# A float16 FFN, plain float32 scores and host-laid inputs in a block-causal attention and gated conv FFN kernel

## The chip, the cores and the metric

The kernel runs on one core of one Trainium2 chip. Its engines are PE (matmul; PEld is its weight load), DVE (vector), ACT (scalar), POOL (GpSimd) and SP, which only issues transfers. The metric is the device time of one execution in microseconds. PE's granted clock is shown in the profile as a share of full speed.

## The reference, cut

```python
# q, k, v: (8 batches, 8 heads, 576 rows, 64);  w_in 512 x 1024, conv_w 3 x 1024, w_out 1024 x 512
scores = scale * np.matmul(q, k.transpose(0, 1, 3, 2))
mask = block_i >= block_j            # blocks of 64 rows: a row sees its own block and those before
scores = np.where(mask, scores, -1000000000.0)
attn = np.exp(scores - max); attn = attn / (sum + 1e-09)
x = (attn @ v), heads side by side   # (8, 576, 512)
h = np.maximum(x @ w_in, 0.0)
conv_out[:, s] = sum over k of conv_w[k] * h[:, s + k - 1]      # zero rows at both ends
gate = 1.0 / (1.0 + np.exp(-conv_out))
return h * gate @ w_out              # (8, 576, 512)
```

The weights arrive as float64 words, so the kernel itself decodes them into float32.

## The kernel before, in words

One program runs on one core. A helper class, `Plan`, first collects every operation (`pl.op`) with its engine, an assumed duration, what it depends on and a target number from a table; `Plan.order` then writes each engine's operations in the order of these numbers, and puts fill matmuls (`work`, L2038) into PE's waits. All eight PSUM banks are given out by it. In it, an operation of DVE marked `port=True` (operands in SBUF) and one of POOL are never planned at the same time.

Heads go in pairs, four to a batch, 32 in all. Batch 0 is done in two parts: "A" (the first 256 rows) and "B" (the rest), both with plain float32 scores (L1477, L1538, L1315), masks by PE (L1481, L1542), and V's product in L1719. The other 28 pairs go whole, with these stages:

- `load_nat` and `load_v`: q, k and v by SP's queue, 64 numbers of a head and row at a time.
- `stage_t`: PE turns q and k (L1166; L1224 in part A), ACT writes the high part in fp32r (L1179, corner of q L1192), DVE the low part (L1182, L1195).
- `stage_s`: three fp32r products per tile (L1391), ACT writes the mask into the bank (L1404), DVE takes maxima (L1413), ACT the exponentials (L1416). `last_s` does the last 64 rows of both heads (L1318, L1321, L1334). `two_planes` writes the normed weights as float16 high (POOL L1271, ACT L1273) and low planes (DVE L1276; for the first tile POOL L1280, L704, L1286). SP turns the planes by transfer (L1297).
- `load_v`: each pair's V is scaled by a power of two, from a sum by ACT (L809), spread by POOL (L812), summed over rows by PE (L815), DVE (L818, L823); then POOL scales it and writes its float16 parts (L829, L704, L835).
- `pair_pv`: the product with V in float16 (L1781), 66 matmuls, two heads side by side; ACT and DVE evict it as high and low parts of x in fp32r (L1789, L1792).
- `ffn`: per batch 8 blocks of w_in, in three products of high and low fp32r parts: FFN-in matmuls (L1824), relu (ACT L1841), the three taps (ACT L1844, DVE L1848, DVE L1852 or ACT L1857 and POOL L1861), tanh (ACT L1864), the gate product (DVE L1867), its high part (ACT L1871 or POOL L704) and low part (POOL L1877), and FFN-out (L1910), evicted by ACT (L1918). A whole batch has two halves, so 16 gate products. A batch's FFN lies beside the attention of the next one.
- `split`: decodes each weight block (DVE L969 to L997) and parts it, for most with two matmuls by an identity (L1048, L1051) and an addition by DVE (L1054). Each block is split as it comes.

## Time and profile before

| | us |
|---|---|
| median of 3 runs (lowest, highest) | 714.97 (714.72, 715.11) |
| span of the profiled execution | 711.6 |
| PE busy | 689.4 |
| DVE busy | 600.5 |
| ACT busy | 589.8 |
| POOL busy | 476.0 |

The span is that of the one profiled execution, from its first to its last instruction. Busy time is the union of an engine's instructions; the chain of waits goes back from the last instruction and says, for each stretch, which engine's work ended last. Matmuls overlap, so the cost of one is the distance between two starts.

### The profile page before, as it was taken

Reading aid. Unit: us, or ns where it says so; the run is one execution under the profiler, and the core shown is the slowest. Engines: PE = TensorE matmul, PEld = TensorE weight load, DVE = VectorE, ACT = ScalarE, POOL = GpSimd, SP = SyncE. Lnnn points to the kernel's source line nnn. Section 1 sums busy time; section 2 is a strip of 40 time slices with the busy share of each in tenths; the row PEclk is TensorE's granted clock in tenths of the full one; section 3 lists DMA queues with packets and bytes.
Section 4 is the critical chain, followed back from the end, with each engine's and each line's share of the span. In section 5 each row is a group of like instructions: output and inputs, shape, how many; then the busy total and the mean of one; then the engine's idle time right before and its main releaser. Section 6 shows DMA issues by size and latency. Waiting matters only on the chain.

```text
span 711.6 us, 17406 instructions
## 1 busy us (share of the span) xinstructions
PE 689.4 (97%) x5824; PEld 575.2 (81%) x5824; DVE 600.5 (84%) x1553; ACT 589.8 (83%) x1859; POOL 476.0 (67%) x716
## 2 busy tenths in 40 slices
PE   8899999998999999999999999999899999999998
PEld 6567778777889788887978888897778879888987
DVE  5999989998888979999988898888998888994441
ACT  6889989897979779798979889997888779884753
POOL 2545285665877758778787758877676767775543
PEclk9999999999999999999999999999999999999999
DMA  8845437699667794957866796877877595574001
GB/s 212 249 101 140 127 63 156 133 184 169 135 133 133 132 178 93 187 111 168 129 133 132 127 183 122 156 143 123 155 125 143 106 192 113 102 141 85 17 29 45
DMA packets 313197, 94.35 MB, mean 133 GB/s; under 512 B 302461, under 2 KB 307605, under 8 KB 313109
## 3 DMA queue, kind: packets, MB, share of 16 engines
q1 hardware_dynamic: 307812, 84.47, 62.1%
q10 hardware_dynamic: 5296, 8.78, 3.8%
q8 instruction: 46, 0.75, 0.4%
q14 instruction: 43, 0.34, 0.2%
HBM read 37.38 MB, written 9.44 MB: 66 GB/s over the span
## 4 chain that ended last, share of the span: by engine, by line
PE 56%; DVE 17%; ACT 16%; issue 3%; POOL 3%; SPq 2%; DMA 2%; ACTq 0%; POOLq 0%; DVEq 0%
PE bank L1910 19%; PE bank L1824 17%; PE bank L1391 5%; PE bank L1781 4%; PE bank L1719 3%; DVE ptbl L1276 3%; DVE su L1413 3%; PE bank L1166 2%; PE bank L1318 2%; ACT t L1864 2%; ACT t L1844 2%; DVE t L1848 2%; ACT bank L1841 1%; DVE t L1867 1%; DVE h L1276 1%
## 5 line engine op out<-in xcount | busy, mean ns | idle before, releaser
L1824 PE MATMUL bank<-x,wih 128*128 128x290 f32 (+3 forms) x1024 | 195.0, 302 | 4.0 <-DVE t L1867 1.8
L1824 PEld LDWEIGHTS bank<-x,wih 128*128 128x128 f32 x1024 | 153.6, 188 | 15.2 <-DVE t L1867 4.3
L1877 POOL TENSOR_TENSOR gl<-t,gh 128x289 fp32r<-128x289 f32 (+3 forms) x128 | 107.7, 845 | 43.0 <-ACT gh L1871 36.9
L1910 PE MATMUL bank<-woh,gh 128*128 128x512 f32 (+1 forms) x296 | 120.0, 406 | 0.1
L1910 PE MATMUL bank<-woh,gl 128*128 128x512 f32 (+1 forms) x296 | 114.8, 388 | 0.0
L1910 PE MATMUL bank<-wol,gh 128*128 128x512 f32 (+1 forms) x296 | 114.5, 387 | 0.0
L1824 PE MATMUL bank<-x,wil 128*128 128x290 f32 (+3 forms) x512 | 108.6, 298 | 0.0
L1413 DVE TENSOR_REDUCE su<-bank 128x1 f32<-128x384 f32 (+3 forms) x224 | 101.2, 481 | 6.7 <-ACT bank L1404 5.9
L1848 DVE SCALAR_TENSOR_TENSOR t<-bank,cw,t 128x286 f32<-128x286 f32 (+3 forms) x128 | 65.4, 512 | 21.9 <-ACT t L1844 18.5
L1824 PEld LDWEIGHTS bank<-x,wil 128*128 128x128 f32 x512 | 81.1, 188 | 1.5 <-issue 0.7
L1867 DVE SCALAR_TENSOR_TENSOR t<-t,bank 128x289 f32<-128x289 f32 (+3 forms) x128 | 56.6, 448 | 16.4 <-ACT t L1864 15.1
L1844 ACT ACTIVATE t<-bank,cw 128x287 f32<-128x287 f32 (+3 forms) x128 | 63.6, 499 | 4.7 <-POOL gl L1877 2.2
L1910 PEld LDWEIGHTS bank<-woh,gh 128*128 128x128 f32 x296 | 55.6, 188 | 13.6 <-issue 3.6
L1910 PEld LDWEIGHTS bank<-woh,gl 128*128 128x128 f32 x296 | 55.6, 188 | 12.1
L1864 ACT ACTIVATE t<-t 128x289 f32<-128x289 f32 (+3 forms) x128 | 55.6, 444 | 10.3 <-DVE t L1852 4.8
L1910 PEld LDWEIGHTS bank<-wol,gh 128*128 128x128 f32 x296 | 55.8, 188 | 7.2
L1841 ACT ACTIVATE bank<-bank 128x288 f32<-128x288 f32 (+3 forms) x128 | 51.2, 403 | 9.7 <-PE bank L1824 9.0
L1271 POOL TENSOR_SCALAR ptbl<-p3f,su 128x512 f16<-128x512 f32 x56 | 43.9, 792 | 11.6 <-DVE su L1436 8.3
L1861 POOL TENSOR_TENSOR t<-t,ptah 128x287 f32<-128x287 f32 (+1 forms) x28 | 25.1, 898 | 39.1 <-DVE t L1848 20.9
L1391 PE MATMUL bank<-kh,qh 64*128 64x384 f32 (+3 forms) x224 | 43.7, 375 | 2.8 <-DVE x L1792 1.5
L1276 DVE SCALAR_TENSOR_TENSOR ptbl<-p3f,su,ptbl 128x512 f16<-128x512 f32 x56 | 46.0, 829 | 0.1
L1416 ACT ACTIVATE p3f<-bank,su 128x512 f32<-128x512 f32 x56 | 38.2, 684 | 6.8 <-DVE su L1413 6.6
(206 smaller groups left out, 1864.3 us busy)
## 6 DMA issues: line engine op xcount, KB each, us to landing
out_dram<-stage ACTq DMA_DIRECT2D x33, 256.0 KB, 3.4
vn<-in_v_dram SPq DMA_DIRECT2D x58, 128.0 KB, 2.8
qnf<-in_q_dram SPq DMA_DIRECT2D x56, 128.0 KB, 2.7
knf<-in_k_dram SPq DMA_DIRECT2D x56, 128.0 KB, 2.8
x<-in_moe_w_out_dram SPq DMA_DIRECT2D x8, 512.0 KB, 3.7
gh<-in_moe_w_in_dram SPq DMA_DIRECT2D x4, 512.0 KB, 5.5
gl<-in_moe_w_in_dram SPq DMA_DIRECT2D x4, 512.0 KB, 4.3
qtf<-in_k_dram SPq DMA_DIRECT2D x32, 32.0 KB, 2.6
```

What stands on the lines that cost most here:

```text
L1271: nc.gpsimd.tensor_scalar(out=hi(), in0=c(tb.ap), scalar1=st.ap[:, col:col + 1], scalar2=0.0, op0=ALU.mult, op1=ALU.add)
L1276: nc.vector.scalar_tensor_tensor(out=lo(), in0=c(tb.ap), scalar=st.ap[:, col:col + 1], in1=hi(), op0=ALU.mult, op1=ALU.subtract)
L1391: nc.tensor.matmul(home[z][hh].ap[:, cols(i)], t[q_].ap[r, 128 * i:128 * i + 128], t[k_].ap[r, 64 + 128 * (3 - i):S], start=(n == 0), stop ...
L1413: nc.vector.tensor_reduce(out=st.ap[:, k:k + 1], in_=sb.ap[:, cols(i)], op=ALU.max, axis=AX.X, negate=True)
L1824: nc.tensor.matmul(fb.ap[:, 0:n2], wt[:, c, fs], xs[c][xi].ap[:, x0:x0 + n2], start=(n + c - c0 == 0), stop=(n + c - c0 == 3 * NCC - 1))
L1841: nc.scalar.activation(out=fb.ap[:, 0:n2], in_=fb.ap[:, 0:n2], func=AF.Relu, scale=0.5 if b == 0 else 2.0 ** -17)
L1844: nc.scalar.activation(out=t.ap[:, 0:no], in_=fb.ap[:, own:own + no], func=AF.Copy, scale=cw[:, NFC + f:NFC + f + 1])
L1848: nc.vector.scalar_tensor_tensor(out=t.ap[:, i0:no], in0=fb.ap[:, own + i0 - 1:own + no - 1], scalar=cw[:, f:f + 1], in1=t.ap[:, i0:no], o ...
L1864: nc.scalar.activation(out=t.ap[:, 0:no], in_=t.ap[:, 0:no], func=AF.Tanh)
L1867: nc.vector.scalar_tensor_tensor(out=t.ap[:, 0:no], in0=t.ap[:, 0:no], scalar=1.0, in1=fb.ap[:, own:own + no], op0=ALU.add, op1=ALU.mult)
L1877: nc.gpsimd.tensor_tensor(out=gbuf[1].ap[:, f, carry:carry + no], in0=t.ap[:, 0:no], in1=gbuf[0].ap[:, f, carry:carry + no], op=ALU.subtract)
L1910: nc.tensor.matmul(fb.ap[:, 0:cut], gbuf[a].ap[:, f, cs], w[:, f, ds], start=(f == 0 and n == 0), stop=(f == NFC - 1 and n == 2))
```

## The change

All six inputs are laid out by the host before the launch: q and k turned, a pair's two heads on 128 partitions, with q's last block of both heads as a block diagonal of 128 columns; v with 640 columns a row; the weights by block. So PE turns nothing for q and k, and a pair's q, k or v comes in one transfer. All scores are plain float32 with PE writing the mask; x, both weights and the gated h are float16 high and low parts; a factor for w_in, one for w_out and one for V of each batch keep them in range. The factor of V is taken per batch by DVE's maximum of each pair (L774), that of each weight over all its eight blocks (L918), so a block is decoded when it comes and split (`split_w`) when the scale is there. Operations may name other engines (`other`); the table's last two bits choose one. The planner lets DVE's `port` operations and POOL's overlap, at a longer duration (`BESIDE`).

```diff
+    BESIDE = 0.4
-                if o.port:
-                    t = max(t, port)
+            if o.port:
+                o.end += self.BESIDE * max(0.0, min(o.end, port[e != POOL]) - t)
+                port[e == POOL] = o.end
...
-    NX = 7
+    NX = 8
-    wih = cp.tile([P, NCC, DFF], F32R, tag="wih", name="wih")
+    wih = cp.tile([P, NCC, DFF], F16, tag="wih", name="wih")
...
     def load_qk(p, at, part=None):
+                eng.dma_start(out=x.ap[:, c], in_=src[b, z, :, c])
...
     def stage_t(nat, at):
+        (xq, lq), (xk, lk) = nat
+        o = scale_q(xq, slice(0, QW), at, lq, POOL)
+        return {"q": xq, "k": xk}, [o, lk], [o, lk]
...
     def stage_s(ops, at):
-                        for n, (q_, k_) in enumerate((("qh", "kh"), ("qh", "kl"), ("ql", "kh"))):
-                            for hh in range(2):
-                                r = slice(64 * hh, 64 * hh + 64)
-                                nc.tensor.matmul(home[z][hh].ap[:, cols(i)], t[q_].ap[r, 128 * i:128 * i + 128],
-                                                 t[k_].ap[r, 64 + 128 * (3 - i):S], start=(n == 0), stop=(n == 2))
+                        for hh in range(2):
+                            r = slice(64 * hh, 64 * hh + 64)
+                            nc.tensor.matmul(home[z][hh].ap[:, cols(i)], t["q"].ap[r, 128 * i:128 * i + 128],
+                                             t["k"].ap[r, 64 + 128 * (3 - i):S], start=True, stop=True)
+                    for hh in range(2):
+                        r = slice(64 * hh, 64 * hh + 64)
+                        x = home[z][hh].ap[0:64, 0:128 * len(tiles)].rearrange("p (j c) -> p j c", c=128)[:, :, 64:128]
+                        nc.tensor.matmul(x, rident[r, r], maskt[r, :].unsqueeze(1).broadcast_to([64, len(tiles), 64]), start=False, stop=True,
+                                         skip_group_check=True)
...
     def load_v(b, at):
+                nc.vector.tensor_reduce(out=sc.ap[:, z:z + 1], in_=vn.ap.rearrange("p c j d -> p (c j d)"), op=ALU.max, axis=AX.X,
+                                        apply_absolute_value=True)
     def split_v(p, at):
+            nc.vector.scalar_tensor_tensor(out=piece(1), in0=src(), scalar=sc.ap[:, 6:7], in1=piece(0), op0=ALU.mult,
+                                           op1=ALU.subtract)
...
     def scale_w(k, at):
+        o, o1 = sums(wm, 16 * k, NFC, at, [wraw[f][2] for f in range(NFC * k, NFC * k + NFC)], [])
     def split_w(f, at):
+        s_, d = ((lambda: fac.ap[:, 2:3]), wdone["a"]) if k == 0 else ((lambda: wm.ap[:, 26:27]), wdone["o"])
+            nc.scalar.activation(out=hi, in_=src(), func=AF.Copy, scale=s_())
+            nc.vector.scalar_tensor_tensor(out=lo, in0=src(), scalar=s_(), in1=hi, op0=ALU.mult, op1=ALU.subtract)
...
     def two_planes(tb, c, n, st, col, hi, lo, bufs, at, deps, pool):
+            return a, pl.op(POOL, c_pool(n, True), h2p, at + 0.6, deps=[a], bufs=[tb, *bufs],
+                            other=((DVE, c_dve(n, two_in=True), partial(h2p, nc.vector), True),))
...
     def ffn(b, o0, o1, xs, at, span):
-            rl = o = pl.op(ACT, c_act(n2) + 0.04, relu, clock, deps=[o, wdone["cw"]], bufs=[fb])
+            rl = o = pl.op(ACT, c_act(n2) + 0.04, relu, clock, deps=[o], bufs=[fb], other=((DVE, c_dve(n2), relu_v),))
-            gdone.append(pl.op(POOL, c_pool(no, True), c6, clock + 3.5, deps=[o] + prev_tail, bufs=[t]))
+            gdone.append(pl.op(POOL, c_pool(no, True), c6, clock + 3.5, deps=[o] + prev_tail, bufs=[t],
+                               other=((DVE, c_dve(no, two_in=True), partial(c6, nc.vector), True),)))
```

PE, scores of a pair of batch 1, before (kh, kl, qh, ql are high and low parts of k and q):

```order
L1391 MATMUL bank<-kh,qh 128x128 x2
L1391 MATMUL bank<-kl,qh 128x128 x2
L1391 MATMUL bank<-kh,ql 128x128 x2
L1391 MATMUL bank<-kh,qh 128x256 x2
L1391 MATMUL bank<-kl,qh 128x256 x2
L1391 MATMUL bank<-kh,ql 128x256 x2
L1391 MATMUL bank<-kh,qh 128x384 x2
L1391 MATMUL bank<-kl,qh 128x384 x2
L1391 MATMUL bank<-kh,ql 128x384 x2
```

PE, the scores of such a pair after (maskt is the mask, rident an identity):

```order
L1171 MATMUL bank<-k,q 128x128 x2
L1171 MATMUL bank<-k,q 128x256 x2
L1177 MATMUL bank<-maskt,rident 64x2x64 x2
L1171 MATMUL bank<-k,q 128x384 x2
L1177 MATMUL bank<-maskt,rident 64x64 x2
L1171 MATMUL bank<-k,q 128x512 x2
L1177 MATMUL bank<-maskt,rident 64x64 x2
```

Three products per tile have become one, and PE's mask matmuls stand behind each bank's tiles.

DVE near the program's start, before (gh is a decoded w_in block, wil its low part, st holds maxima of the first scores):

```order
L997 SCALAR_TENSOR_TENSOR wil<-gh 128x4x128
L1570 TENSOR_REDUCE st_151<-st_151 128x4
L990 TENSOR_SCALAR gh<-gh 128x512
L1574 RECIPROCAL st_151<-st_151 128x4
L997 SCALAR_TENSOR_TENSOR wil<-gh 128x4x128
L1054 TENSOR_TENSOR wil<-bank,gh 128x4x128
L1753 TENSOR_TENSOR x<-bank,x 64x256
```

DVE there after, where the last w_in maximum (wm) is taken and the scale is made:

```order
L1334 TENSOR_REDUCE st_150<-bank 128x1 x2
L1348 TENSOR_REDUCE st_148<-st_148 128x4
L881 SCALAR_TENSOR_TENSOR wf<-raw,wf 128x512
L1352 RECIPROCAL st_148<-st_148 128x4
L1281 TENSOR_REDUCE st_144<-st_144 128x2
L719 TENSOR_REDUCE vs<-bank 128x1
L918 TENSOR_REDUCE wm<-raw 128x1
L1286 RECIPROCAL st_144<-st_144 128x2
L724 TENSOR_SCALAR vs<-vs 128x1
L709 TENSOR_REDUCE wm<-wm 128x1
L734 TENSOR_SCALAR wm<-wm 128x1
L884 TENSOR_SCALAR raw<-wf 128x512
```

The low part of a block no longer follows its decoding; the maxima, the scale and softmax maxima of batch 0 stand between.

POOL, V's scale and parts for a pair of a later batch, before (vn is V as loaded, vs its scale, vx its float16 parts):

```order
L812 TENSOR_SCALAR dg<-ident,vs 128x128
L704 TENSOR_SCALAR gh<-t 128x287
L1877 TENSOR_TENSOR gl<-t,gh 128x287
L829 TENSOR_SCALAR vn<-vn,vs 128x640
L704 TENSOR_SCALAR vx<-vn 128x640
L835 TENSOR_TENSOR vx<-vn,vx 128x640
```

POOL there after (vb takes V's parts, p0f and p1f are exponentials, ptbl the planes):

```order
L813 TENSOR_SCALAR vb<-vn,vs 128x640
L1055 TENSOR_SCALAR p1f_110<-p1f_110,su_158 128x256
L1055 TENSOR_SCALAR p0f_106<-p0f_106,su_158 128x128
L1061 TENSOR_SCALAR ptbl<-p1f_110 128x2x128
L1061 TENSOR_SCALAR ptbl<-p1f_112 128x2x128
L1061 TENSOR_SCALAR ptbl<-p0f_106 128x128
L1045 TENSOR_SCALAR ptbl<-p2f_116,su_158 128x3x128
L1067 TENSOR_TENSOR ptbl<-p0f_106,ptbl 128x128
```

One pass over V is left on POOL, and the second tile's planes have come to it from ACT and DVE.

## Rows read from the trace of the kernel before

**Rows 1.** The page: busy us and share by engine; shares of the chain

```profile
PE 689.4 (97%) x5824; PEld 575.2 (81%) x5824; DVE 600.5 (84%) x1553; ACT 589.8 (83%) x1859; POOL 476.0 (67%) x716
...
PE 56%; DVE 17%; ACT 16%; issue 3%; POOL 3%; SPq 2%; DMA 2%; ACTq 0%; POOLq 0%; DVEq 0%
```

**Rows 2.** Busy us by engine and stretch; PE clock, DMA share, GB/s

```profile
0.00:20.00 20.00, 17.78 (x101) 12.51 (x102) 11.22 (x41) 13.70 (x41) 6.52 (x17) 1.00 0.82 211
20.00:36.00 16.00, 13.65 (x77) 7.86 (x76) 15.60 (x43) 13.92 (x45) 8.73 (x14) 1.00 0.87 249
...
60.00:140.00 80.00, 78.88 (x552) 60.62 (x551) 75.68 (x201) 73.18 (x230) 46.41 (x69) 1.00 0.56 125
...
400.00:480.00 80.00, 80.00 (x728) 69.14 (x728) 70.63 (x193) 71.46 (x233) 59.82 (x91) 1.00 0.79 150
480.00:560.00 80.00, 75.79 (x700) 64.67 (x697) 72.34 (x180) 66.79 (x215) 58.59 (x90) 1.00 0.72 132
```

**Rows 3.** Timeline of DVE, 32nd and 112th gate product; start, length

```profile
245.77 0.46 DVE L1867 SCALAR_TENSOR_TENSOR t<-t,bank 128x289 f32<-128x289 f32 x1 [0.24 <-ACT t L1864]
...
647.32 0.82 DVE L1867 SCALAR_TENSOR_TENSOR t<-t,bank 128x289 f32<-128x289 f32 x2
```

**Rows 4.** Chain of waits in the tail; start, length, what

```profile
658.48 12.88 PE bank L1824 x96
```

**Rows 5.** Timeline of PE in a steady cycle; start us, length us, engine, line

```profile
412.97 0.37 PE L1166 MATMUL bank<-rident,knr 128*128 128x128 f32 x3
413.18 0.47 PE L1910 MATMUL bank<-woh,gh 128*128 128x512 f32 x1
413.48 0.40 PE L1910 MATMUL bank<-wol,gh 128*128 128x512 f32 x1
413.72 0.40 PE L1910 MATMUL bank<-woh,gl 128*128 128x512 f32 x1
...
415.21 0.55 PE L1781 MATMUL bank<-ptbh,vv 128*64 128x256 f16 x8
415.59 0.32 PE L1781 MATMUL bank<-t,vv 128*64 128x64 f16 x10
```

**Rows 6.** Chain of waits, steady: fp32r scores of a pair, last block

```profile
415.92 2.10 PE bank L1391 x24
...
448.19 0.99 PE bank L1318 x6
```

**Rows 7.** Timeline of PE in the head, plain float32 scores and masks

```profile
46.60 1.13 PE L1477 MATMUL bank<-kh,qh 64*128 64x512 f32 x4
...
47.69 0.50 PE L1048 MATMUL bank<-wih,nident 128*128 128x512 f32 x1
```

**Rows 8.** Chain of waits in the head

```profile
36.07 0.74 PE bank L1824 x4
...
61.78 1.17 PE bank L1315 x4
...
64.04 3.18 PE bank L1719 x16
```

**Rows 9.** DVE groups by line and shape; busy us, mean ns

```profile
L1413 DVE TENSOR_REDUCE su<-bank 128x1 f32<-128x512 f32 x56 | 37.5, 683 | 2.5 <-ACT bank L1404 2.4
...
L1276 DVE SCALAR_TENSOR_TENSOR ptbl<-p3f,su,ptbl 128x512 f16<-128x512 f32 x56 | 46.0, 829 | 0.1
...
L1276 DVE SCALAR_TENSOR_TENSOR ptbl<-p1f,su,ptbl 128x256 f16<-128x256 f32 x56 | 32.8, 593 | 2.5 <-ACT ptbl L1273 2.4
...
L1182 DVE SCALAR_TENSOR_TENSOR kl<-bank,kh 128x192 fp32r<-128x192 f32 (+1 forms) x56 | 24.9, 448 | 1.1 <-ACT qdh L1192 0.4 <-ACT kh L1179 0.3 <-ACT qh L1179 0.3
```

**Rows 10.** Timelines of DVE (first two) and of POOL; start, length

```profile
111.30 0.74 DVE L1276 SCALAR_TENSOR_TENSOR ptbl<-p3f,su,ptbl 128x512 f16<-128x512 f32 x1
...
648.06 1.00 DVE L1276 SCALAR_TENSOR_TENSOR ptbl<-p3f,su,ptbl 128x512 f16<-128x512 f32 x1
...
647.71 0.81 POOL L1877 TENSOR_TENSOR gl<-t,gh 128x289 fp32r<-128x289 f32 x1 [1.43 <-ACT gh L1871]
```

1010 lines of the change are left out of this document (407 added, 603 removed), and 354 rows, old and new, of the table TARGETS.

## The prediction

> **What bounds the kernel now.** I read the page first, then the busy time by stretches, then the chain of waits, and last the timeline of the places that the change touches. The page says that PE is busy 97% of the span and carries 56% of the chain, DVE and ACT 17 and 16% [rows 1]. The stretches split the program in two. Up to 140 us DVE is busy 75.7 of 80 us and PE's time holds fill matmuls; from 240 us on, one batch repeats every 80.4 us (the 32nd and the 112th gate product stand 401.9 us apart, five batches [rows 3]), PE is busy 75.8 to 80.0 of 80 and DVE 70.6 to 72.3 [rows 2]. So there are three sections: a head up to 245.8 us in which DVE and PE both are near full, five cycles of 80.4 us bound by PE with some 2 us of holes each, and a tail from 647.7 us to the end of pure FFN. The profiled span is 711.6 us against a median of 715.0 of the runs: 3.4 us lie outside it, which I add at the end.
>
> **PE, term by term.** All prices are spacings, start to start, since a matmul's own duration overlaps the next.
>
> FFN in float16: 1536 FFN-in matmuls of some 289 columns and 840 of 512 plus 48 of 256 columns FFN-out, 886,000 columns. Now 96 in a row take 12.88 us [rows 4], 0.464 ns a column; FFN-out runs at 0.24 us for 512 [rows 5], 0.46. Float16 is in the trace at V's product: 8 matmuls, two side by side, 896 columns, take 0.38 us [rows 5], 0.424 ns a column, with weight loads of half the width. At 0.43 the FFN takes 381 us where it took some 406: **-25**. From below -30 (0.424); from above 0, if the separate weight load of 128 columns shows. I take the row because its matmuls are nearly as long as these. The Trainium skill ("TensorE: Matmul & The Clock Gate", Back-to-back issue gap) gives N/2.4 + 2.5 ns for a lone stream, which would make this term -31 and the time 678; no row has a full-width float16 matmul.
>
> Transposes of q and k by PE go (272 in the whole pairs and rests, 16 in the first parts): three take 0.21 us and the matmul behind them starts 0.07 late [rows 5], 0.093 each: **-27**, at least -20 without the turn. The identity matmuls that split the weights go: 32 at 0.24: **-8**. The scale of V needs 10 all-rows sums in place of 28 (of a transposition's size): **-2**. V's product in batch 0 takes 3.18 us for a pair's second part [rows 8]; with two heads side by side this halves, four times, and the first parts give a little: **-7** (0 to -10).
>
> Scores: a pair's 24 products in fp32r take 2.10 us, the six of the last block 0.99 [rows 6]. Plain float32 is in the head: 512 columns of two heads take 1.09 us, their masks by PE included [rows 7]. A pair has 128, 256, 384 and 512, 2.5 times as many columns: 2.73, and up to 3.05 as three mask matmuls a head stand in it where 2.5 would by that scale, and short runs carry more of the switch; nearer 2.8. That is +0.7 for each of 28 pairs, **+20** (18 to 27, and 14 if one mask matmul for two tiles costs as one). The last block costs 1.17 [rows 8] in place of 0.99, or less where other work doesn't cut the six in two: **+7** (5 to 10). PE now writes the masks, and ACT no longer does. Fills rise from 39 to 67, nearly all before the first FFN cycle is over: **+7**, in the head alone, where PE waits anyway.
>
> Sum on PE: -25 - 27 - 8 - 2 - 7 + 20 + 7 + 7 = **-35**. Of a steady cycle (192 FFN-in, 111 FFN-out, four pairs): FFN -3.1, transposes -3.3, sums -0.3, scores +2.9, last block +1.0, together **-2.8**.
>
> **DVE.** What goes: 112 low parts of q and k, of which the k half is 24.9 us and the q half alike, 56 low planes of 256 columns, 32.8 us [rows 9], the 56 corners of q, 16 additions behind the identity matmuls and 84 small ones of the V scale (those some 40 by their sizes). That is about 120 us of its records. What comes: 32 maxima over 640 columns of V and 16 over 512 of the weights, at 0.683 for 512 [rows 9] 0.85 and 0.68: 38. Low parts of V, 28 at 640 columns, by the 0.829 of 512 some 0.95: 27. Low parts of the weights 16 x 0.83: 13. The planner's choice of engine puts some relu, high copies, low copies and evictions of the FFN and high planes on DVE, some 110 operations of 0.3 to 0.5: 45. Sum +123: by these DVE ends +3, and since the choices were counted at their lower durations I take **+8** (-5 to +25) higher, +1 in a cycle. ACT gives up the high parts of q and k, the masks and V's sums, about 11 us a cycle; POOL gives up the three passes over V (now one, or none) and takes low planes instead.
>
> **The head** is where the change adds a wait. Each weight block used to be split as it came; now the scale needs the maximum of all eight FFN-in blocks, so no block is split before the eighth has landed and its maximum has gone through POOL, PE and DVE. The first FFN-in matmul starts at 36.07 us now [rows 8]. With q, k and V of batch 0 queued ahead, about 8 MB must land; at the 211 and 249 GB/s of the first two stretches [rows 2] that is 32 to 38 us, and 3.5 for the chain: 36 to 42. Behind the waiting split on DVE stand the softmax maxima of batch 0, which the order places ahead of it, so DVE keeps work. DVE is nearly full up to 140 us [rows 2] and gets no lighter there (the 16 maxima and low parts, 24 us, against 11 of additions and the low parts of q and k), while PE loses identity matmuls, half of V's product, transposes and two batches' FFN gain, some 23, and gets the fills back as 7. Bounds for the head: -16 (PE decides) and +7 (DVE decides); I take **-8**, since from 140 us on PE decides again.
>
> **Sum.** Head -8. Cycles: -2.8 from PE's work and -1 of the 2 us of holes, because the chain's ACT links (evictions, masks) get shorter: five times -3.8, **-19**. Tail: 192 FFN-in and about 150 FFN-out matmuls at the gain above, **-3.5**. The span becomes 711.6 - 30.5 = 681, the time **684.5**. Own range of this case 674 to 696.
>
> **Rivals.**
> 1. *PE's holes close.* PE can be busy 80.0 of 80 [rows 2]; if ACT's relief keeps it so, and the scores come at their lower end, a cycle is 74: five times -6.4, head -14, tail -5: **664**. For it: ACT falls most. Against it: DVE would be 72.5 of 74.
> 2. *DVE becomes the bound, or the weight load shows.* DVE is busy 71.5 a cycle, gets 1, and in the head it has run no fuller than 95% [rows 2]: 72.5 / 0.95 = 76.3, just under the forecast's 76.6; 2.5 more, by contention (next rival), make it 79: five times -1.4, head 0, tail -3.5: **704**. With no FFN gain the forecast loses 25: **709**.
> 3. *Slower: DVE and POOL hold each other up.* The planner before kept operations with SBUF operands on DVE and POOL apart; now it lets them overlap. The same 512-column low plane takes 0.74 us alone and 1.00 us while POOL subtracts [rows 10]: +0.26. A cycle will have some 33 DVE operations with two SBUF inputs; if all are hit that is +8.6, DVE 81, the cycle 85. It decides from 4 us on: (72.5 + 4) / 0.95 = 80.5. With 70% hit, the cycle is 82.6: +11, head +2, tail -3: **725**. Against it: POOL's busy time falls, and rows before already hold such hits. The Trainium skill ("SBUF — State Buffer", SBUF: two separate sides) has the pair of ports as a lock, the loser blocked until the other's instruction ends; by it a hit would cost half of POOL's 0.81, 33 times, and the cycle would pass 88 us. The trace agrees only in part: in that row 0.46 us of POOL's operation were left and the plane lost 0.26.
>
> **How the numbers follow.** Forecast 0.48, rival 1 0.20, rival 2 0.21, slower 0.09, and 0.02 for the strip between. 0.2% (1.4 us) is about what a measurement of this kernel can tell from no change. Faster 0.88, same 0.03, slower 0.09. Below 658 I leave 0.08, above 710 about 0.11: the range is 658 to 710, which takes in FFN at its old rate and scores at either end.
>
> **What would show it.** In the profile after: FFN-in runs of 96 at 0.123 to 0.125 us each (right) or 0.134 (wrong); a pair's score run with masks at 2.8 us; no transposes by PE behind the head; the first FFN-in matmul at 36 to 42 us; gate products 16 apart by 76 to 77 us for two halves of a batch in the steady state; DVE busy 72 to 74 of each cycle. If DVE is above 95% there, rival 2 holds; if low planes average over 1.0 us, rival 3. A first FFN-in matmul past 50 us would sink the head's term.

## The result and the profile after

The changed kernel takes 680.74 us, the median of four runs from 678.58 to 681.38. The kernel before takes 714.85 us on the same chip (714.43 to 715.11). The ratio is 0.9522, with a 95% interval of 0.950 to 0.9543: faster by 4.8%, or 34 us. The profiled execution of after took 680.9 us with a span of 679.1. The forecast was 684.5, with a range of 658 to 710.

From the page of after: busy us and share by engine; the TensorE clock in 40 slices, in tenths; the DMA packets. They answer to [rows 1].

```profile
PE 639.0 (94%) x5402; PEld 403.1 (59%) x5402; DVE 621.9 (92%) x1542; ACT 501.4 (74%) x1440; POOL 432.6 (64%) x646
...
PEclk9889779999999999999999999999999999999999
...
DMA packets 205505, 95.13 MB, mean 140 GB/s; under 512 B 185308, under 2 KB 187636, under 8 KB 205428
```

PE lost 50.4 us of busy time and the span lost 32.5. ACT lost 88.4, POOL 43.4. DVE alone gained, 21.4.

Busy time of after by stretches: from:to and length, then PE, PEld, DVE, ACT and POOL, the granted clock, DMA share and GB/s. It answers to [rows 2].

```profile
20.00:36.00 16.00, 13.11 (x76) 8.11 (x72) 15.97 (x43) 8.76 (x31) 14.28 (x22) 0.89 0.47 172
36.00:60.00 24.00, 20.04 (x120) 12.49 (x120) 23.55 (x59) 20.06 (x51) 19.60 (x20) 0.86 0.39 128
60.00:140.00 80.00, 69.01 (x492) 43.10 (x490) 77.44 (x188) 63.05 (x172) 61.86 (x79) 0.91 0.39 107
...
400.00:480.00 80.00, 78.44 (x703) 48.75 (x702) 76.73 (x193) 64.10 (x189) 52.38 (x85) 1.00 0.75 160
480.00:560.00 80.00, 79.67 (x755) 50.05 (x754) 77.17 (x199) 62.98 (x183) 48.33 (x75) 1.00 0.68 140
```

In the steady stretches PE is still 98 to 100% busy, but DVE is now at 96%, where it was at 88 to 90% [rows 2]. From 20 to 140 us PE is less busy than before, and its granted clock is 0.86 to 0.91 of the full level, where before it was 1.00.

For a comparison of the sections I take the starts of the 384th and the 1344th FFN-in matmul in either trace. They bound the head, five batches of 192 matmuls, and the tail, from the first busy instruction to the last, which is some 3 us less than the span. Per cycle, "DVE idle" is the cycle less DVE's busy time.

The prediction bounded its sections by the 32nd and the 112th gate product instead. The row at 647.32 that it calls the 112th, a row of two products, holds the 110th and 111th; the 112th is 4 us later. That was a slip: by its own marks a cycle before is 81.1 us, not 80.4. The 112th of before, then the 32nd and 112th of after, answer to [rows 3] (timeline of DVE; start, length):

```profile
651.52 0.46 DVE L1867 SCALAR_TENSOR_TENSOR t<-t,bank 128x289 f32<-128x289 f32 x1 [1.92 <-ACT t L1864]
...
241.53 0.44 DVE L1565 SCALAR_TENSOR_TENSOR t<-t,bank 128x289 f32<-128x289 f32 x1
...
621.82 0.46 DVE L1565 SCALAR_TENSOR_TENSOR t<-t,bank 128x289 f32<-128x289 f32 x1 [1.45 <-ACT t L1562]
```

In the table, before, after and the first difference go by FFN-in matmuls, the second difference by gate products.

| | before | after | measured | by gate products | forecast |
|---|---|---|---|---|---|
| first FFN-in matmul, us | 35.8 | 41.8 | +6.0 | | 36 to 42 |
| head | 231.2 | 235.4 | +4.2 | -4.2 | -8 |
| one cycle | 82.3 | 75.2 | -7.1, five: -35.6 | -5.1, five: -25.5 | -3.8, five: -19 |
| tail | 66.1 | 64.9 | -1.2 | -2.8 | -3.5 |
| sum | | | -32.6 | -32.5 | -30.5 |
| cycle: PE busy | 80.5 | 73.6 | -6.9 | -4.9 | -2.8 |
| cycle: DVE busy, idle | 73.6, 8.7 | 72.0, 3.2 | -1.6, -5.5 | +0.3, -5.4 | +1 |
| cycle: ACT busy | 70.8 | 58.7 | -12.1 | -10.5 | -11 |
| cycle: POOL busy | 61.1 | 47.7 | -13.4 | -12.3 | less |

The two kernels order the FFN differently beside the attention, so where the head ends depends on the mark; by the 385th and 1345th FFN-in matmul the three differences are -2.3, -29.9 and -0.4. What holds by every mark: the head gave less than the forecast 8 us (between 4.2 shorter and 4.2 longer), the five cycles gave more than the forecast 19 (25 to 36), and 5.5 us a cycle of DVE's idle time went. So the sum was met by terms that missed in both directions.

What DVE waited for in either kernel, from 240 to 600 us: the waiting operation, the one waited for, us in total, times, longest. Before:

```profile
DVE su L1413 <- ACT bank L1404: 5.7, 8, 1.8
DVE su L1346 <- ACT p4f L1334: 4.1, 9, 1.1
DVE x L1792 <- ACT x L1789: 4.0, 6, 1.1
DVE t L1848 <- ACT t L1844: 3.8, 11, 0.7
DVE t L1867 <- ACT t L1864: 3.8, 12, 0.6
DVE h L1276 <- ACT h L1273: 2.2, 3, 1.0
```

After:

```profile
DVE t L1546 <- ACT t L1542: 1.6, 5, 0.6
DVE su L1127 <- ACT p4f L1115: 1.6, 3, 0.6
DVE stage L1623 <- PE bank L1610: 1.5, 2, 0.8
DVE ptbl L1051 <- ACT ptbl L1048: 1.4, 2, 1.0
DVE t L1565 <- ACT t L1562: 1.3, 3, 0.6
```

Before, the long waits are all for ACT, the mask write (L1404) first. After, no item reaches 2 us. These rows gave the second theory below; the prediction had not read what DVE waits for.

### The profile page after: what moved, and what is told of

Read it like the earlier page. It is cut to its first block, busy times and chain, and to the rows that moved or that the text cites. A ratio compares the mean times of both kernels' runs of the same rounds, so it can differ in the third digit from the quotient of the medians.

```text
span 679.1 us, 15540 instructions
## 1 busy us (share of the span) xinstructions
PE 639.0 (94%) x5402; PEld 403.1 (59%) x5402; DVE 621.9 (92%) x1542; ACT 501.4 (74%) x1440; POOL 432.6 (64%) x646
## 5 line engine op out<-in xcount | busy, mean ns | idle before, releaser
L1521 PE MATMUL bank<-x,wih 128*128 128x290 f16 (+3 forms) x1024 | 177.6, 289 | 7.9 <-DVE x L1482 3.8
L1521 PEld LDWEIGHTS <-wih 128*128 128x128 f16 x1024 | 98.2, 99 | 47.3 <-issue 13.4
L1576 POOL TENSOR_TENSOR gl<-t,gh 128x287 f16<-128x287 f32 (+3 forms) x109 | 88.8, 819 | 39.0 <-ACT gh L1569 22.5
L1610 PE MATMUL bank<-woh,gh 128*128 128x512 f16 (+1 forms) x296 | 110.9, 375 | 1.1 <-DVE x L1482 0.7
L1610 PE MATMUL bank<-woh,gl 128*128 128x512 f16 (+1 forms) x296 | 110.5, 373 | 0.1
L1610 PE MATMUL bank<-wol,gh 128*128 128x512 f16 (+1 forms) x296 | 110.5, 373 | 0.0
L1521 PE MATMUL bank<-x,wil 128*128 128x290 f16 (+3 forms) x512 | 102.9, 290 | 0.5 <-DVE wil L949 0.5
L1191 DVE TENSOR_REDUCE su<-bank 128x1 f32<-128x384 f32 (+3 forms) x224 | 100.0, 479 | 1.1 <-PE bank L1177 0.4
L1171 PE MATMUL bank<-k,q 64*128 64x384 f32 (+3 forms) x448 | 82.1, 468 | 1.9 <-ACT p4f L1115 1.1
L1542 ACT ACTIVATE t<-bank,cwb 128x287 f32<-128x287 f32 (+3 forms) x128 | 63.4, 500 | 16.8 <-POOL gl L1576 11.3
L1471 PEld LDWEIGHTS <-vb 128*64 128x64 f16 x1848 | 62.8, 112 | 19.5 <-issue 17.9
L1546 DVE SCALAR_TENSOR_TENSOR t<-bank,cwb,t 128x286 f32<-128x286 f32 (+3 forms) x128 | 64.4, 507 | 7.1 <-ACT t L1542 5.8
L1565 DVE SCALAR_TENSOR_TENSOR t<-t,bank 128x287 f32<-128x287 f32 (+3 forms) x128 | 56.1, 444 | 5.3 <-ACT t L1562 5.1
```

Source lines behind the costliest of these rows:

```text
L1171: nc.tensor.matmul(home[z][hh].ap[:, cols(i)], t["q"].ap[r, 128 * i:128 * i + 128], t["k"].ap[r, 64 + 128 * (3 - i):S], start=True, stop=True)
L1191: nc.vector.tensor_reduce(out=st.ap[:, k:k + 1], in_=sb.ap[:, cols(i)], op=ALU.max, axis=AX.X, negate=True)
L1471: nc.tensor.matmul(tb.ap[64 * j:64 * j + 64, c0:c1], vb.ap[:, w, c, j, :], x, start=first, stop=(z == 1 and c == jobs[-1][0]), skip_group_ ...
L1521: nc.tensor.matmul(fb.ap[:, 0:n2], wt[:, c, fs], xs[c][xi].ap[:, x0:x0 + n2], start=(n + c - c0 == 0), stop=(n + c - c0 == 3 * NCC - 1))
L1542: nc.scalar.activation(out=t.ap[:, 0:no], in_=fb.ap[:, own:own + no], func=AF.Copy, scale=cwb.ap[:, NFC + f:NFC + f + 1])
L1546: nc.vector.scalar_tensor_tensor(out=t.ap[:, i0:no], in0=fb.ap[:, own + i0 - 1:own + no - 1], scalar=cwb.ap[:, f:f + 1], in1=t.ap[:, i0:no ...
```

## The experiments

Theory A is the prediction's: in the cycles PE decides. Theory B is that the cycle is a chain through queues that run in order, above all through DVE, so that its length is DVE's work plus what DVE waits, mostly for ACT. For the head, theory H1 is that the wait for all eight w_in blocks costs the time, H2 that DVE's added work does, H3 that DVE and POOL hold each other up. The order and the choice of engines are kept in each experiment unless its text says otherwise, so these runs tell what decides under the given order; a table tuned anew might use the freed time better.

Each kernel is compared with the kernel before on its own chip (medians 714.9, 716.4, 716.3 and 715.7 us); "by the savings" means by the difference of these comparisons. The rows carry the names of the runs, which are taken up one by one below. The sections are found by the FFN-in matmuls, each from one profiled execution. Those of e13_halfmax_nowil, e1_const and e4_before_nowil lie 3.5, 2.1 and 1.9 us under their medians, the others within some 1.4 us of theirs. Between kernels of the same order the choice of marks moves a difference of cycles by 0.4 us at most.

| kernel | time, us | saved against before, us | ratio, 95% | head | cycle | tail | per cycle: PE | DVE | DVE idle |
|---|---|---|---|---|---|---|---|---|---|
| after | 680.74 | 34.1 | 0.950 to 0.954 | 235.4 | 75.2 | 64.9 | 73.6 | 72.0 | 3.2 |
| e1_const | 680.89 | 35.5 | 0.948 to 0.955 | 231.7 | 75.5 | 64.9 | 73.7 | 72.0 | 3.5 |
| e2_nomax | 680.57 | 35.8 | 0.948 to 0.956 | 234.2 | 75.2 | 64.9 | 73.6 | 72.0 | 3.2 |
| e3_pool8 | 678.99 | 37.4 | 0.945 to 0.952 | 234.1 | 75.3 | 64.9 | 73.6 | 71.9 | 3.4 |
| e4_after_nowil | 675.64 | 40.8 | 0.941 to 0.947 | 234.0 | 74.8 | 63.5 | 67.8 | 71.8 | 3.0 |
| e12_halfmax | 669.15 | 47.2 | 0.933 to 0.936 | 229.5 | 73.9 | 64.9 | 73.0 | 66.7 | 7.2 |
| e13_halfmax_nowil | 660.27 | 56.1 | 0.921 to 0.925 | 226.9 | 72.4 | 62.9 | 66.8 | 66.3 | 6.1 |
| e5_vsum_act | 686.90 | 28.8 | 0.958 to 0.963 | 240.0 | 75.7 | 64.9 | 73.8 | 70.3 | 5.4 |
| e10_mask_act | 697.08 | 18.6 | 0.972 to 0.979 | 235.8 | 78.0 | 65.3 | 74.0 | 72.2 | 5.8 |
| before | 714.85 | 0 | | 231.2 | 82.3 | 66.1 | 80.5 | 73.6 | 8.7 |
| e4_before_nowil | 706.68 | 9.6 | 0.984 to 0.989 | 228.4 | 81.9 | 62.1 | 75.0 | 73.5 | 8.4 |
| e7_before_f16 | 706.72 | 9.6 | 0.984 to 0.989 | 231.3 | 81.8 | 62.8 | 77.5 | 73.8 | 8.0 |
| e14_before_nomask | 712.48 | 3.2 | 0.994 to 0.998 | 230.8 | 82.0 | 66.2 | 80.3 | 73.5 | 8.5 |
| e15_before_f16_nomask | 699.06 | 16.6 | 0.975 to 0.981 | 228.4 | 80.8 | 62.8 | 77.0 | 73.4 | 7.4 |

### Is PE the bound of the cycles? PE's work taken away in either kernel

The product with w_in's low part (`wil`) is left out of FFN-in, a third of its matmuls; everything on the other engines stays.

```diff
                     def mm(wt=wt, xi=xi, c0=c0, n=n, fb=fb, fs=fs):
+                        if wt is wil:
+                            return
                         for c in (c0, c0 + 1):
```

> The changed kernel without the product of x's high part and the weights' low part: 512 of 1536 FFN-in matmuls are left out, 64 to 66 us of PE's work, 8 us of each batch. If PE alone decides the steady part, a cycle falls by 8 (to 68) and the time to 625 to 632. If DVE is the next bound (76.5 of 80 us busy in the stretches from 240 us on), a cycle can only fall to DVE's 72 to 73: the time stays at 655 to 665.

> The kernel before without the product of x's high part and the weights' low part: 512 of 1536 FFN-in matmuls are left out, some 68 to 72 us of PE's work. If PE bounds the kernel before, the time falls until DVE bounds it (71.4 us a cycle, full at 95 to 96%: 75): by 35 to 50, to 665 to 680. If DVE or a chain held the kernel before as it holds the changed one, it falls by under 12.

After fell by 5.1 us (6.7 by the savings on each chip), before by 9.6. Busy time by stretches of before with the product left out (columns as above):

```profile
400.00:480.00 80.00, 75.83 (x674) 62.13 (x673) 72.06 (x195) 73.17 (x240) 59.58 (x90) 1.00 0.75 146
480.00:560.00 80.00, 70.57 (x632) 58.10 (x631) 71.20 (x180) 66.74 (x213) 59.82 (x91) 0.98 0.70 134
```

And of after with the product left out:

```profile
400.00:480.00 80.00, 73.02 (x646) 43.96 (x644) 77.19 (x190) 65.14 (x190) 52.47 (x84) 0.98 0.76 160
480.00:560.00 80.00, 73.93 (x687) 44.20 (x684) 77.74 (x200) 63.08 (x185) 47.88 (x73) 0.98 0.69 143
```

PE lost 5.5 us of busy time a cycle in before (80.5 to 75.0) and 5.8 in after (73.6 to 67.8), and the cycle lost 0.4 in both (0.3 and 0.0 by gate products). Under theory A it would have lost most of it. PE's busy time simply fell to 88 to 95% of the same stretch, at a granted clock of 0.98 to 1.00. Of what before gained, 4.0 us are in the tail, which is pure FFN. **Theory A falls, for the kernel before as well**: PE at 100% of an 80 us stretch [rows 2] was full and yet did not decide. One sign of why is in the busy time itself: the matmuls left out were priced at 64 to 72 us, but PE's busy time fell by 45 and 46 us, because those left stand farther apart (FFN-in 0.158 us each in before, where it was 0.142). A matmul of FFN-in counts as busy for its own 0.30 us even when the next one comes late, so part of PE's busy time was waiting.

### Is DVE? Its maxima on half of the columns

The softmax maxima of the scores (L1104, L1191) read half of the columns. The shift that is subtracted is then the maximum of that half.

```diff
-                nc.vector.tensor_reduce(out=st4.ap[:, j:j + 1], in_=sb.ap[:, 0:HS], op=ALU.max, axis=AX.X)
+                nc.vector.tensor_reduce(out=st4.ap[:, j:j + 1], in_=sb.ap[:, 0:HS // 2], op=ALU.max, axis=AX.X)
...
-                            nc.vector.tensor_reduce(out=st.ap[:, k:k + 1], in_=sb.ap[:, cols(i)], op=ALU.max, axis=AX.X, negate=True)
+                            nc.vector.tensor_reduce(out=st.ap[:, k:k + 1], in_=sb.ap[:, cols(i)][:, 0:64 * (i + 1)], op=ALU.max, axis=AX.X, negate=True)
```

> The changed kernel with the softmax maxima of the whole pairs and the last blocks taken over half of their columns, so half of each such scan on DVE is left out: DVE loses some 45 us, 5.3 of each batch; nothing else changes. Taking a third of FFN-in from PE had brought 5 us only. If DVE alone bounds the steady part, a cycle falls by 5 and the time to 645 to 652. If PE stands close behind it (78.5 of 80 us busy), the cycle falls by 1 to 2 and the time to 668 to 675. If neither does and a chain through the in-order queues does, it stays at 678 to 681.

> Both at once: half of the softmax maxima left out on DVE, and the product with the weights' low part left out on PE. If DVE and PE bound the steady part together, each hiding the other, a cycle falls by 5 and the time to 635 to 650, far more than the sum of the two alone. If a chain through several engines bounds it, the time is the sum of the two alone or less: 665 to 675.

The second is this edit together with the missing product. DVE's work fell by 5.3 us a cycle and the cycle by 1.3; the head fell by 5.9, and the whole by 11.6 (13.1 by the savings). This is the outcome that was expected with PE close behind DVE. The largest wait of DVE from 240 to 600 us is then one for PE's scores:

```profile
DVE su L1191 <- PE bank L1177: 4.5, 13, 0.9
```

With both edits the cycle fell by 2.8 and the whole by 20.5 (22.0 by the savings), somewhat more than the two apart add up to (5.1 and 11.6, or 6.7 and 13.1). That meets neither of the two outcomes expected, the sum or less and the far larger fall. PE is then busy 66.8 and DVE 66.3 of 72.4 us, so even the two together don't set the cycle. So a microsecond of DVE's work is worth more than one of PE's, some 0.25 against 0.07 a cycle, but neither engine alone decides: when DVE has less to do, its idle time rises from 3.2 to 7.2. That fits a chain through several in-order queues, and it speaks for theory B in its weak form only: what shortens the cycle is work or waits on the chain, wherever it runs.

### Does ACT's relief matter? Masks back to ACT, V's bound to ACT, masks taken from before

The mask of the scores goes back from PE to ACT, as a write of its own ahead of the DVE maximum, and is placed in ACT's row by the planner's time for the end of the scores; the rest of the order stays.

```diff
-                        nc.tensor.matmul(x, rident[r, r], maskt[r, :].unsqueeze(1).broadcast_to([64, len(tiles), 64]), start=False, stop=True,
-                                         skip_group_check=True)
...
+                    def mk(sb=sb, tiles=tiles):
+                        x = sb.ap[0:64, 0:128 * len(tiles)].rearrange("p (j c) -> p j c", c=128)[:, :, 64:128]
+                        nc.scalar.activation(out=x, in_=maskt[0:64, :].unsqueeze(1).broadcast_to([64, len(tiles), 64]).bitcast(F32), func=AF.Copy)
...
+                    mo = pl.op(PE, 0.001, mk, t0, deps=[o], bufs=[sb], other=((ACT, 0.055 + 0.06 * len(tiles), mk),))
...
-                        e = pl.op(DVE, c_dve(128 * i + 128), mx, t0 + 0.3 + OSH * hh, deps=[o], bufs=[sb, st])
+                        e = pl.op(DVE, c_dve(128 * i + 128), mx, t0 + 0.3 + OSH * hh, deps=[mo], bufs=[sb, st])
```

> The changed kernel with the masks of the whole pairs written by ACT again (the mask instructions as in the kernel before, put into ACT's order where the planner has the scores end) and not by PE: PE loses some 36 us, ACT gets 36 more. If ACT in DVE's chain is what the change removed, DVE's waits return and the time rises by 4 to 12, to 685 to 693. If PE's work sets the steady part, it falls by 4 to 8, to 673 to 677.

697.08 us: 16.3 us of the 34 are gone again (15.5 by the savings), more than the 4 to 12 expected; in the profiled execution 14 of 14.7 are in the five cycles. ACT's work rose by only 3.6 us a cycle, to 62.3 of 78.0. PE got little in return: its busy time per cycle rose from 73.6 to 74.0, and the scores without masks take 75.6 us in all, where scores and masks took 80.8. What DVE waited for, 240 to 600 us, in this kernel:

```profile
DVE su L1203 <- ACT bank L1194: 12.2, 21, 1.7
DVE su L1138 <- ACT p4f L1126: 1.7, 3, 0.8
```

The first row is the maximum that waits for the mask: 12.2 us over 4.6 cycles, 2.6 a cycle, and the cycle is 2.8 longer. Here the price of the step is the wait on DVE, not ACT's time, which had room. One reservation: ACT's row was not tuned for this write, and the planner put 9 more fill matmuls into PE's waits, so 16 is likely an upper end for what the masks on PE are worth.

In the other direction V's bound is taken by ACT, as a sum of magnitudes, and no longer by DVE's maximum; it too is placed in ACT's row by the planner's time:

```diff
+            def most_a(vn=vn, z=z):
+                nc.scalar.activation(out=junk.ap, in_=vn.ap.rearrange("p c j d -> p (c j d)"), func=AF.Abs, scale=2.0 ** -9,
+                                     accum_out=sc.ap[:, z:z + 1])
...
-            maxs.append(pl.op(DVE, c_dve(640), most, at + 3 + 0.5 * z, deps=[ld], bufs=[vn, sc]))
+            maxs.append(pl.op(DVE, c_dve(640), most, at + 3 + 0.5 * z, deps=[ld], bufs=[vn, sc, junk], other=((ACT, 0.83, most_a),)))
```

> The changed kernel with the bound of V for its factor taken by ACT as a sum of absolute values (32 times some 0.8 us, as the kernel before did for each pair) and not by DVE as a maximum: DVE loses 26 us (3.2 of each batch), ACT gets 28. If DVE sets the steady cycle (72.0 of 75.2 us busy), and ACT with 58.7 has room, a cycle falls by 0.5 to 1.5 as with half of the softmax maxima (-1.3 for 5.3) and the time by 5 to 9, to 672 to 676. If ACT's place in DVE's chain matters more, it stays or rises by up to 4.

686.90 us, 6.2 slower (5.3 by the savings), although 32 operations of 0.80 us left the fullest engine. DVE's work fell by 1.7 us a cycle and ACT's rose by 1.8, and the cycle is 0.5 longer; the head is 4.6 longer. Its waits on DVE:

```profile
DVE t L1580 <- ACT t L1577: 5.3, 7, 1.1
DVE ptbl L1066 <- DMA ptbx<-ptbl: 3.3, 3, 1.5
DVE t L1561 <- ACT t L1557: 3.3, 7, 1.4
```

The convolution's steps on DVE (t) wait for ACT again, as they did in before. Under this order, work moved from an engine at 96% to one at 78% made the kernel slower: the receiver stands in the chain too. The planner also put 11 more fill matmuls into PE's waits, 8 of them in the head, so the head's part may not be ACT's alone.

Last, the masks are taken out of the kernel before, once alone and once together with float16 (below). These two leave out the mask.

```diff
                     def mk(sb=sb, tiles=tiles):
+                        return
                         x = sb.ap[0:64, 0:128 * len(tiles)].rearrange("p (j c) -> p j c", c=128)[:, :, 64:128]
```

> The kernel before without ACT's mask writes into the score banks (168 instructions, 36 us of ACT): the mask of the whole pairs is left out, the maxima wait for PE alone. In the kernel before a steady cycle of 82.3 us holds 73.6 us of DVE's work and 8.7 in which DVE waits, nearly all for ACT; in the changed kernel 72.0 and 3.2. If ACT's place in DVE's chain set the cycle, the waits fall by 2 to 4 a cycle and the time by 10 to 20, to 696 to 706. If PE's queue (97% busy) set it, nothing on PE changed: under 4 less.

712.48 us: only 3.2 us, although the wait for L1404 was the largest on DVE. By its own words the expectation gives this outcome to PE's queue. But the missing product excluded PE's queue as the cycle's bound, and the waits of DVE, 240 to 600 us, show another reason:

```profile
DVE x L1793 <- ACT x L1790: 5.2, 6, 1.5
DVE t L1849 <- ACT t L1845: 5.0, 13, 1.0
```

The waits moved on to the next operations of ACT (these two had 4.0 and 3.8), and DVE's idle time is 8.5 us a cycle, where it was 8.7. ACT had 67.5 us to do in a cycle of 82.0, so the engine had room; that its operations came late by their place in ACT's row is the reading that fits, but no run moves them. So the masks cost 16 us where they are put into after, and 3 where they are taken out of before. Neither figure is "the price of the masks"; it depends on what else is late.

### The float16 FFN alone

The FFN of before with x, the weights and the gated h in float16 (the types of the tiles and of the identities that split the weights); layout, scores, V and order stay.

```diff
-    wih = cp.tile([P, NCC, DFF], F32R, tag="wih", name="wih")
+    wih = cp.tile([P, NCC, DFF], F16, tag="wih", name="wih")
...
-    gbuf = [Buf(cp, [P, NFC, GW], F32R, tag) for tag in ("gh", "gl")]
+    gbuf = [Buf(cp, [P, NFC, 2 * GW], F16, tag) for tag in ("gh", "gl")]
...
-        x = pl.buf(px, [P, 2, S], F32R, "x", NX)
+        x = pl.buf(px, [P, 2, 2 * S], F16, "x", NX)
```

> The kernel before with one part of the change alone: weights, x and gated h as float16 high and low parts, and nothing else (scores, transposes, V, weights and the order stay; no factors keep the parts in range, so low parts lose bits). FFN matmuls should take 38 us less of PE, as in the changed kernel. If PE bounds the kernel before, the time falls by 22 to 35, to 680 to 693, and most of the change's gain is this part. If the gain needs the other parts (transposes, identity matmuls, ACT's relief), it falls by under 12.

706.72 us, 9.6 less. The sections of its profiled execution, whose span is 6.0 shorter, say where: 3.3 in the tail, 0.5 in each cycle (0.9 by gate products), nothing in the head. PE's work fell by 3.0 a cycle and by 4.4 in the tail. Three quarters of PE's gain arrive where the program is only FFN, and a sixth to a third in the cycles.

> Both on the kernel before: float16 FFN (alone -9.6 us) and no mask writes by ACT. If PE and ACT each hold the cycle where the other is relieved, the two together bring more than their sum: 28 to 35 less, 681 to 688, close to the whole change. If they act apart, the sum of the two alone.

Float16 and no mask together: 699.06 us, 16.6 less, somewhat more than 9.6 and 3.2 and far from the 28 to 35 expected if PE and ACT hid each other. This is the nearest that I came to after from before's side. Its cycle is still 80.8 us and DVE still waits 7.4 of it. So of the 34.1 us that after saved, some 17.5 belong to what this kernel lacks: the layout by the host (no transposes and splits of q and k, whose high parts were ACT's and low parts DVE's work), plain float32 scores, V's scale by batch, the choice of engines and the new order. That half was not taken apart further, since its parts share the operations whose order the table sets; no run tells what a new order alone would have brought.

### What keeps the head from gaining

First the wait: the split of the weights by constants, so that no block waits for the eighth.

```diff
-        s_, d = ((lambda: fac.ap[:, 2:3]), wdone["a"]) if k == 0 else ((lambda: wm.ap[:, 26:27]), wdone["o"])
+        s_ = (lambda: kf[:, 0:1]) if k == 0 else (lambda: kf[:, 1:2])
...
-        o = pl.op(ACT, c_act(512, False, True), fh, at, deps=[o, d], bufs=[g, fac, wm],
+        o = pl.op(ACT, c_act(512, False, True), fh, at, deps=[o], bufs=[g],
```

> The changed kernel, but the factors by which w_in and w_out are split are two constants written at the start, so no block's split waits for the maxima of all eight; the maxima and their chain still run, the order on every engine stays. If the wait for the eighth block decides the head (a first FFN-in matmul at 42 us where it was at 36), that matmul goes back to some 36 to 37 us and the time from 680.7 to 675 to 677. If DVE's work decides it, the split finds DVE busy anyway: the time stays within 1.5 us of 680.7.

680.89 us: no change within the intervals (the head of its profiled execution is 3.7 us shorter, but that was its shortest run, 2.1 under the median). The first FFN-in matmul stands at 41.5 us instead of 41.8. The wait is there in the program, but under this order the eighth block isn't what is late. H1 falls.

Then DVE's work: beside the constants, the 16 maxima of the weights read 8 of their 512 columns.

```diff
-            nc.vector.tensor_reduce(out=wm.ap[:, c:c + 1], in_=words(1).bitcast(F32), op=ALU.max, axis=AX.X, apply_absolute_value=True)
+            nc.vector.tensor_reduce(out=wm.ap[:, c:c + 1], in_=words(1)[:, 0:8].bitcast(F32), op=ALU.max, axis=AX.X, apply_absolute_value=True)
```

> As the kernel with constant factors, and the 16 maxima of the weights take 8 of 512 columns (0.68 us becomes some 0.15), which leaves out nothing else of DVE's work: DVE loses some 8.5 us, all of it in the first 110 us. If DVE decides the head, the time falls by 7 to 9, to 672 to 674; if the wait or PE's lower clock decides it, it stays where the constant factors alone put it.

680.57 us: again no change, although DVE has 7.4 us less to do in the head (223.5 to 216.1). The stretch of 60 to 140 us of this kernel, against 77.44 of DVE above:

```profile
60.00:140.00 80.00, 69.39 (x489) 43.12 (x488) 74.29 (x188) 63.20 (x173) 61.45 (x78) 0.91 0.40 106
```

H2, in the form that DVE's amount of work alone sets the head, falls: the freed 3 us are idle there, and PE does hardly more (69.4 us against 69.0).

Then the meeting of DVE and POOL. In after there are short operations of DVE that last until POOL's end. DVE's timeline (start, length, line, operation):

```profile
25.15 1.28 DVE L888 SCALAR_TENSOR_TENSOR cr<-cr 24x128 f32<-24x128 uint32 x1
...
51.88 1.18 DVE L783 TENSOR_SCALAR cwb<-cwa,vs 128x24 f32<-128x24 f32 x1
```

POOL's at the same places:

```profile
25.01 1.28 POOL L891 TENSOR_TENSOR wf<-wf,raw 128x512 f32<-128x512 f32 x1
...
51.31 1.71 POOL L891 TENSOR_TENSOR wf<-wf,raw 128x512 f32<-128x512 f32 x1
```

Twenty-four columns take 1.18 us (0.22 at the shortest, of eight runs of this line), and both DVE operations end within 0.2 us of POOL's. I summed what each DVE operation takes over the short end (10th percentile) of its own kind, counting what is 50 ns or more. It is 9.8 us in the first 240 us of before and 21.4 in after, so 11.6 more, 7.8 of them in the first 140 us; in the 400 us behind it is 33 and 34. Every one of these operations in the first 240 us overlaps one of POOL's. The experiment cuts the POOL operation at both places to 8 of 512 columns, which leaves out the low word of the decoded weights.

```diff
-            eng.tensor_tensor(out=g(), in0=g(), in1=words(1).bitcast(F32), op=ALU.add)
+            eng.tensor_tensor(out=g()[:, 0:8], in0=g()[:, 0:8], in1=words(1)[:, 0:8].bitcast(F32), op=ALU.add)
```

> The changed kernel, but POOL's addition of the two parts of each decoded weight block (16 times 1.28 us) takes 8 of 512 columns, so the low word of most weights is left out; DVE's operations are the same. If collisions with POOL stretch DVE in the head (its operations there are 11.5 us longer than alone, 3.8 before the change), the stretch falls by a third to a half and the time by 3 to 6, to 675 to 678. If DVE's own work or the wait for the factors decides, it stays within 1.5 us of 680.7.

678.99 us, 1.8 less (3.3 by the savings; the two intervals overlap, so this stays unclear). By the same sum DVE's meetings fell from 21.4 to 15.5, POOL's work in the head by 19 and the head by 1.3. The stretch of 36 to 60 us, against 23.55 of DVE and 19.60 of POOL above:

```profile
36.00:60.00 24.00, 19.48 (x110) 12.25 (x110) 19.16 (x55) 18.39 (x46) 12.07 (x17) 0.79 0.36 118
```

DVE has nearly 5 of the 24 us free, and PE does no more than before the edit: H3 isn't the whole either. **What holds the head stays open.** The runs exclude the wait for the factors, DVE's maxima alone and half of the meetings alone as the single cause. Halving the softmax maxima shortened the head by 5.9 us, taking V's bound to ACT made it 4.6 longer; so the softmax chain of the first batches, over DVE and ACT, is likely in it. One candidate was not tested, PE's own clock. From 20 to 140 us its mean is 0.90 in after and 1.00 in before, and only 0.87 in the execution of e3_pool8 (0.79 in the row shown last), so PE may have done no more there because it ran slower. Among the four runs of e1_const the shortest has the highest clock and the longest the lowest (678.81 us at 0.985, 682.69 at 0.972); which of the two follows from the other isn't shown.

## Why the prediction was right, and where it was not

The time was right (680.7 against 684.5, well inside the range), and its sign. Its mechanism was half right: two errors of the sum offset each other, which was luck. By the prediction's own marks the head gave 3.8 us less and the cycles 6.5 more than forecast. A smaller miss is the 3.4 us that it added for what lies outside the span: in after's profiled execution it is 1.8 us (680.9 less 679.1).

**The step that failed: "five cycles of 80.4 us bound by PE".** It read a busy share of 95 to 100% [rows 2] as a bound. PE's gain was then priced as time. The experiments show that 5.5 us a cycle less on PE gave 0.4 in before. The forecast's cycle of -3.8 was thus the right order for a wrong reason. On DVE the cycle's gain is 5.5 us less waiting by every mark, and 1.6 less to 0.3 more work. That DVE's waits for ACT can set the cycle is shown by the masks put back (2.8 us a cycle); that the whole gain comes this way is argued, not shown. The prediction had it in a single clause (-1 of the holes, "because the chain's ACT links (evictions, masks) get shorter") and sized it five times too small; it had not read what DVE waits for. ACT's own fall was right: 11 forecast, 10.5 to 12.1 measured. The sign that it gave for the cycle was met as well, gate products 76 to 77 us apart: measured are 76.1.

**PE's terms**, as spacings, were mostly right in size, even though they were not what counted. I give each matmul the time from its start to the next one's, and no more than its own duration. Scores, FFN-in and FFN-out of after in PE's timeline (start, length, count at the end):

```profile
329.82 0.93 PE L1171 MATMUL bank<-k,q 64*128 64x128 f32 x8
...
332.43 0.57 PE L1471 MATMUL bank<-ptbh,vb 128*64 128x256 f16 x8
...
335.66 1.14 PE L1521 MATMUL bank<-x,wih 128*128 128x288 f16 x8
336.64 0.41 PE L1521 MATMUL bank<-x,wil 128*128 128x288 f16 x2
...
349.02 0.38 PE L1610 MATMUL bank<-woh,gh 128*128 128x512 f16 x1
...
350.74 0.38 PE L1610 MATMUL bank<-woh,gl 128*128 128x512 f16 x1
```

And runs in the chain of waits near its end (start, length, what):

```profile
606.81 0.97 PE bank L1101 x4
...
629.85 12.63 PE bank L1521 x102
...
661.22 14.64 PE bank L1610 x90
```

- FFN in float16: 102 FFN-in matmuls take 12.63 us, 0.124 each, where it was 0.134 [rows 4]; eight FFN-out matmuls follow one another in the 1.72 us from 349.02 to 350.74, 0.215 each, where it was 0.24 [rows 5]. Over all, FFN-in fell from 217.6 to 196.9 us and FFN-out from 209.6 to 191.9: -38 where -25 stood. The float16 side was nearly right, 381 forecast and 389 measured. The mis-sized side was before's: some 406 (its own prices give 409) where the spacings sum to 427, mostly since FFN-in costs 0.142 a matmul with its switches and not the 0.134 of the unbroken run. The formula of the Trainium skill ("TensorE: Matmul & The Clock Gate", Back-to-back issue gap), which the prediction set beside its rate, gives an estimate of 215.8 ns for 512 columns and 122.5 for 288; the rows give 215 and, for the eight from 335.66 to 336.64, 122.5. Within a run it was the better guide. In the same section the Trainium skill gives the formula for a single matmul by itself and a shorter 131 ns at 512 columns for a stream with weight loads; these rows, each matmul with its own weight load, show the former and not the latter.
- Transposes of q and k and identity matmuls: 26.7 and 10.3 us to nothing; forecast -27 and -8.
- Scores: a pair's run goes from 329.82 to 332.43, 2.61 us with its masks, against 2.10 [rows 6]; forecast 2.8, with 2.6 as its lower end. In sum +14 (66.9 to 44.6 and 36.2 for masks) where +20 stood. The last block costs 0.97 in the row shown and 1.17 on average, +6.8 in sum; forecast 1.17 and +7.
- V's product in batch 0: -10.7, forecast -7. Fills +10, forecast +7. All of PE: -50, forecast -35.

**DVE**: forecast +8 in all, measured +21: by gate products +9 in the head, +0.3 a cycle, +10 in the tail, where the planner gave it work that hides beside the FFN. By form the terms were near. DVE's groups of after (busy us, mean ns):

```profile
L1051 DVE SCALAR_TENSOR_TENSOR ptbl<-p3f,su,ptbl 128x512 f16<-128x512 f32 x56 | 46.6, 843 | 0.8 <-POOL ptbl L1045 0.6
...
L774 DVE TENSOR_REDUCE vs<-vn 128x1 f32<-128x640 f32 x32 | 25.4, 804 | 0.0
...
L918 DVE TENSOR_REDUCE wm<-raw 128x1 f32<-128x512 f32 x16 | 10.5, 675 | 4.2 <-DMA raw<-in_moe_w_in_dram 4.2
```

V's maxima cost 0.80 (forecast 0.85), those of the weights 0.675 (0.68). In the first 240 us DVE is busy 13.4 us longer than before, and 11.6 of that are longer meetings with POOL.

**The head** (-8, measured -4.2 by gate products and +4.2 by FFN-in matmuls) was mis-sized because it supposed that "from 140 us on PE decides again" and took PE's net gain of 16 us as worth half. PE did lose 15 to 23 us of busy time there (by FFN-in matmuls 221.1 to 206.5), and by every mark its idle time rose by some 19. The first FFN-in matmul was right at the edge (42.05 us in the profile's time, forecast 36 to 42), and the wait for the eighth block, whose price the section worked out, decides nothing. DVE went from 89 to 95% of the head. (Rival 2 says that DVE in the head ran no fuller than 95% [rows 2]; its row from 20 to 36 us has 15.60 of 16.00, 97.5%.)

**The tail** (-3.5): float16 alone gave 3.3, as forecast. After's own tail is 2.8 shorter by gate products and 1.2 by FFN-in matmuls, behind which 9 more FFN-out matmuls stand than in before.

**The rivals.** The first (PE's holes close, 664) didn't come; PE's work would have allowed it. The second had the cycle right: DVE 72.5 us at 95% gives 76.3, and measured are 72.5 of 76.1 by gate products, 72.0 of 75.2 by FFN-in matmuls. But the prediction set 704 as its price, by contention that would lift DVE further, and that didn't come: its sign (DVE above 95% in the cycles) was met and its time was not. The third (DVE and POOL collide, 725) didn't come in the cycles, where the 512-column low planes average 0.843 us against 0.829 [rows 9]. It did come in the head, as 11.6 us on DVE, half of which could be taken away for only 1.8 us of time. The Trainium skill ("SBUF — State Buffer", SBUF: two separate sides) has the loser blocked to the end of the other's instruction; the short operations at 25.15 and 51.88 us agree with that, more plainly than the planes of [rows 10] did.

## What to carry to other kernels

A busy share of 97% names the engine that is full, which need not be the one that decides: before pricing an edit by it, look at what the next engines wait for in order, and if there is a chip, take 5 us of that engine's work away and see. Where queues run in order, judge a cycle by an engine's work plus its waits; an edit that takes an operation out from between two others of that chain is worth its wait at most, and less where the next operation is late too; one that moves work to a less busy engine can cost more than it frees, if that engine stands in the chain too. An edit's price alone and its price with the others differ (3 and 16 us for the same masks), so a sum of terms can meet the time while its terms do not. And where two kernels order their work differently, bound the sections by more than one mark before saying which of them gained: here the head's sign turned with the mark.
